# Attention beside an MLP: two steps at a time, with projections and turned output in one stretch of the TensorE and all transposes in another

## The chip, the cores and the metric

The kernel runs on one core of a Trainium2 chip. The metric is the device time of one execution in microseconds. Five engines work side by side, each through its own instructions in order: TensorE (PE) multiplies, VectorE (DVE), ScalarE (ACT) and GpSimd (POOL) do the rest of the arithmetic, and SyncE (SP) issues nearly all DMA transfers. Matmul results land in PSUM, which has eight banks of 128 x 512 floats. POOL does not touch PSUM here.

## The reference, cut to what matters

```python
def phi(x):                                   # random features of one row of q or k
    proj = einsum('bhsd,md->bhsm', x, omega)
    h = proj - sum(x * x) / 2
    return exp(h - max(h)) / sqrt(m)
kv  = einsum('bhsm,bhsd->bhmd', phi(k), v)
z   = sum(phi(k), axis=2)
num = einsum('bhsm,bhmd->bhsd', phi(q), kv)
den = einsum('bhsm,bhm->bhs', phi(q), z) + 1e-06
x   = (num / den) as [B * S, H * D]
out = (silu(x @ w_gate) * (x @ w_val)) @ w_out
```

There are 8 batches, 8 heads, 576 rows, head width 64, 128 features; the MLP has 4608 tokens, width 512 and inner width 1536. Everything is fp32.

## The kernel before, in words

The heads are taken in pairs, so that 128 partitions hold two heads. The rows of a batch are nine groups of 256. A *step* `n` takes two groups: one of q and one of k, but only k in the first six steps and only q in the last six (66 to 71). There are 72 steps, and 4 more in which the last results come out.

A step goes through these stages, several steps apart, and the program's names are used in the profile too:

- `st_transpose`: four transposes (`pt`) turn the loaded rows (`nat`), ACT copies them to `x`; POOL squares them (`sq`).
- `st_project`: `pp`, eight matmuls with 64 rows each, for two heads that lie in the two halves of the array's rows. Two tiles, one for each head, take two PSUM banks.
- `st_max`: DVE sums `sq`, takes the maxima of `pp` and makes the bias (`st`). `st_exp`: ACT takes eight exponentials from `pp` to `ph`.
- `k_accumulate`: `kvacc` sums phi(k) x v in one bank; at a batch's half `kv_finalize` copies it to `kvr` and, from batch 4 on, transposes z (`zp`), which goes to DRAM (`zd`) and comes back to all partitions (`zt`).
- `q_transpose`: `ptq`, four transposes of phi(q), copied to `qt`.
- Batches 0 to 3: `q_mult` makes `po` (numerator and denominator), DVE divides (`xn`), `q_out` transposes that to `xt`. Batches 4 to 7: POOL and DVE make the denominator from `zt` (`jk`, `dj`), POOL divides phi(q) (`q_norm`), and `q_out` makes `xt` at once as *turned output*, from two matmuls of 64 columns in the two halves of the array's columns.
- ACT copies `xt` out: to the MLP's input `xh`/`xl`, or through `xo` and a DMA to DRAM (`xs`).

From step 25 on (`EARLY`) the MLP runs beside this. Its matmuls (`g`, `v`, `o`, 128 x 128 x 512, three for each product of split numbers) are given out in shares: `course` says how much of it is due by each step, and each `SHARE` in the list of a step gives an equal part of what is due. Before, the list for one step is `GROUPED`, with six shares. A scheduler settles the final order on each engine; the lists give it the program's order.

PSUM is held by pools: `ps_m` three banks (`ps_moe`), `ps_p` two (`ps_proj`), and one each for `ps_a` (`ps_att`), `ps_b` (`ps_tr`) and `ps_k` (`kvacc`). In the stretch beside the MLP, `pp` is in `ps_proj`, `pt` in `ps_tr`, `ptq` and `xt` in `ps_att` or `ps_tr`, `po` and `zp` in `ps_att`.

After step 75 these pools are given back and the rest of the MLP runs alone (`pair_rounds`), from about 565 us of the span to its end.

Of the kernel before, what the change touches and what calls it, by code (L numbers as in the profile page):

```python
# [24 lines left out]
def kernel(  # L25
# [404 lines left out]
    def st_transpose(n):  # L430
        if n >= NS:
            return
        nat = nats.pop(n)
        pt = ps_tr(f"pt_{n}", [P, 2, G])
        for i in range(2):
            for c in range(CH):
                turned_in[:] = [
                    transpose(
                        pt[:, i, c * P : (c + 1) * P], nat[:, i, c].rearrange("p h d -> p (h d)"), ident
                    )  # L440
                ]
        x = att.tile([P, 2, G], F32, name=f"x_{n}", tag="x")

        st = att.tile([P, 4, 2, CH, 2], F32, name=f"st_{n}", tag="st", bufs=6)
        sq = att.tile([P, 2, CH, 2, D], F32, name=f"sq_{n}", tag="sq")
        nc.gpsimd.tensor_tensor(sq, nat, nat, op=ALU.mult)  # L446
        if 3 <= n < EARLY:
            nc.scalar.copy(x[:, 0], pt[:, 0])
            nc.vector.tensor_copy(x[:, 1], pt[:, 1])
            for w in (D // 2, D // 4):  # L450
                lower_, upper_ = (sq[..., o : o + w].rearrange("p i c h d -> p (i c h) d") for o in (0, w))
                nc.gpsimd.tensor_tensor(lower_, lower_, upper_, op=ALU.add)
        else:
            nc.scalar.copy(x, pt)  # L454
# [42 lines left out]
    def st_exp(n):  # L497
        if n >= NS:
            return
        st, _, pp = sts.pop(n)  # L500
        for i, (kind, b, g) in enumerate(steps[n]):
            ph = att.tile([P, CH, 2 * M], F32, name=f"ph{i}_{n}", tag=f"ph{i}", bufs=3)
            for hh in range(2):
                for c in range(CH):
                    step_end["s"] = nc.scalar.activation(  # L505
                        ph[:, c, hh * M : (hh + 1) * M], pp[hh][:, i, c, :],
                        AF.Exp, bias=st[:, 3, i, c, hh : hh + 1], scale=1.0,
                    )
            box[kind, b, g] = ph
        return True  # L510
# [7 lines left out]
    def kv_finalize(b, a2):  # L518
        acc = kvacc.pop((b, a2))
        raw = att.tile([P, 4, VW], F32, name=f"kvr{b}_{a2}", tag="kvr", bufs=4)  # L520
        nc.scalar.copy(raw, acc)  # L521
        for j in range(2):
            kvst[b, 2 * a2 + j] = raw[:, 2 * j : 2 * j + 2, :]
        if b >= BPOOL:

            zp = ps_att(f"zp{b}_{a2}", [4, P])
            transpose(zp, raw[:, :, D], ident)
            zs = att.tile([4, P], F32, name=f"zs{b}_{a2}", tag="zs")
            nc.scalar.copy(zs, zp)
            zd = dram.tile([4, P], F32, name=f"zd{b}_{a2}", tag="zd", bufs=4)  # L530
            nc.sync.dma_start(zd, zs)
            zds[b, a2] = zd

    zds = {}
    zbc = {}

    def load_z(n):
# [12 lines left out]
    def q_den(n):  # L550

        n -= JLAG
        for _, b, g, gr in slots(n, "q"):
            if b < BPOOL:
                continue
            ph = box["q", b, g].rearrange("p c (h m) -> p c h m", m=M)
            jk = att.tile([P, CH, 2, M], F32, name=f"jk{b}_{g}", tag="jx")
# [12 lines left out]
            dn = att.tile([P, 3, CH, 2], F32, name=f"dj{b}_{g}", tag="dj", bufs=6)  # L570
# [51 lines left out]
    def q_transpose(n):  # L622
# [2 lines left out]
        todo += [(b, g) for _, b, g, gr in slots(n - NLAG, "q") if b >= BPOOL]  # L625
        for i, (b, g) in enumerate(todo):
            ph = box.pop(("q", b, g))
            pt = (ps_moe if m < EARLY else ps_tr if i else ps_att)(f"ptq{b}_{g}", [P, 2, G])
            for hh in range(2):
                for c in range(CH):  # L630
                    transpose(pt[:, hh, c * P : (c + 1) * P], ph[:, c, hh * M : (hh + 1) * M], ident)
# [3 lines left out]
    def q_mult(n):  # L635

        n -= MLAG
        for _, b, g, gr in slots(n, "q"):
            if b >= BPOOL:
                continue  # L640
            qt = qts.pop((b, g))
            po = ps_att(f"po{b}_{g}", [P, CH, 2, VW])
# [14 lines left out]
            xn = att.tile([P, CH, 2, D], F32, name=f"xn{b}_{g}", tag="jx")  # L657
            nc.vector.tensor_tensor(
                xn.rearrange("p c h d -> p (c h) d"),
                po[:, :, :, 0:D].rearrange("p c h d -> p (c h) d"),  # L660
# [10 lines left out]
    cols_done = [0]  # L671

    def q_out(n):
        n -= OLAG
        for i, b, g, gr in slots(n, "q"):
            po = (ps_att if n + OLAG < EARLY or i else ps_tr)(f"xt{b}_{g}", [P, G])
            first = column(b, gr)
            if b < BPOOL:
                xn = xns.pop((b, g))
# [2 lines left out]
            else:  # L682
# [437 lines left out]
    def turn_next(n):  # L1120
# [17 lines left out]
    GROUPED = (
        q_out,
        st_project,  # L1140
        q_transpose,
        lambda n: k_accumulate(n, 0),
        lambda n: k_accumulate(n, 1),
        st_max,
        st_exp,
        q_den,
        lambda n: st_transpose(n + 1),
        SHARE,
        SHARE,
        SHARE,  # L1150
        lambda n: q_norm(n + 1),
        q_mult,
        SHARE,
        SHARE,
        SHARE,
    )

    for n in range(2):
# [8 lines left out]
    warm(2, turned_in[0])  # L1167
    loaded = 3
    ends = []
    for n in range(NN):  # L1170
        if loaded <= n + LA:
            load(loaded)
            loaded += 1
# [6 lines left out]
        want = OPS * np.interp(clock[n + 1], [clock[m] for m, _ in marks], [x for _, x in marks])  # L1180
        order = CLOSE if n < EARLY else GROUPED
        left = len(order) if n < EARLY else order.count(SHARE)
        for what in order:
            with ExitStack() as es:
                if n < EARLY:
                    for ins in ends if what is st_project else ends[:1]:
                        es.enter_context(tc.issue_after(ins.ins))
                if what is not SHARE:
                    what(n)
            if n < EARLY:  # L1190
                if what is st_project:
                    ends.clear()
                ends.append(newest_pe[0])
            if what is turn_next and n < 2:
                warm(2, turned_in[0])
            if n < EARLY or what is SHARE:
                due = course[n + 1] - given[0] - debt[0]
                if due > 0:
                    give(due / left)
                for _ in range(int(np.ceil((want - ticks[0]) / left))):  # L1200
                    tick()
                left -= 1
# [42 lines left out]
```

## Time and profile before

| | |
|---|---|
| median of 3 runs | 1166.98 us (1164.1 to 1167.11) |
| profiled execution | 1166.82 us, span 1165.0 us |
| PE busy | 1137.2 us, 98% of the span |
| DVE, ACT, POOL busy | 61%, 58%, 53% |
| granted TensorE clock, mean | 0.997 |
| attention alone | 0 to about 112 us |
| attention beside the MLP | about 112 to 565 us |
| MLP alone | about 565 to 1165 us |

In a timeline of PE, each row is a run of equal matmuls: start, length, line, tiles and count. The end of a matmul is modelled and overlaps the next; so the distance from one start to the next is the cost, not the length. An fp32 matmul that isn't a transpose is shown as two. In a list of waits, the first name waited for the second.

### The profile page before, as it was taken

The page shows a single profiled execution, that of the slowest core. Times are in us where ns is not written, and L with a number is a line of the kernel's source. Part 1 is how long each engine was busy: PE and PEld are TensorE (multiplying, and loading weights), DVE is VectorE, ACT ScalarE, POOL GpSimd, SP SyncE. Part 2 cuts the span into 40 slices and gives each one's busy share as a digit, 9 for nine tenths or more (in the row PEclk, how much of TensorE's full clock was granted, in tenths as well). Part 3 has the DMA queues.
Part 4 walks back from the last instruction along what each step waited for, and adds up shares of the span by engine and source line. Part 5 has one row for each costly group of instructions (what it writes and reads, how often), then busy time and mean ns, then how long its engine had stood idle before and what let it go on. Part 6 is the DMA issues. An engine that isn't in the chain of part 4 may idle for free.

```text
span 1165.0 us, 18915 instructions
## 1 busy us (share of the span) xinstructions
PE 1137.2 (98%) x6645; PEld 939.5 (81%) x6646; DVE 707.4 (61%) x1289; ACT 678.3 (58%) x1539; POOL 615.5 (53%) x559
## 2 busy tenths in 40 slices
PE   8999999999999999989999999999999999999998
PEld 6888888888878778867788778888878888888886
DVE  5787667455656656565474566665566666456654
ACT  5887886876776866757434544454544445444441
POOL 5664433344556675587245555544455543455551
PEclk9999999999999999999999999999999999999999
DMA  6764445655445642322544111124211111211103
GB/s 137 179 160 114 128 142 161 178 135 143 122 126 137 168 132 78 114 68 65 154 118 126 46 55 55 55 74 122 59 55 55 54 37 46 81 55 55 46 19 72
DMA packets 173966, 114.30 MB, mean 98 GB/s; under 512 B 125840, under 2 KB 144304, under 8 KB 173872
## 3 DMA queue, kind: packets, MB, share of 16 engines
q1 hardware_dynamic: 172528, 112.78, 35.5%
q8 instruction: 52, 0.85, 0.3%
q10 hardware_dynamic: 1344, 0.33, 0.1%
q14 instruction: 42, 0.34, 0.1%
HBM read 87.88 MB, written 25.18 MB: 97 GB/s over the span
## 4 chain that ended last, share of the span: by engine, by line
PE 74%; DVE 10%; ACT 6%; POOL 4%; DMA 3%; issue 2%; SPq 1%; ACTq 0%; POOLq 0%; DVEq 0%
PE o L103 22%; PE a L103 16%; PE c L103 8%; PE g L103 6%; PE pp L103 4%; PE v L103 4%; PE d L103 4%; PE kvacc L103 3%; ACT ph L505 3%; PE ptq L107 2%; PE po L103 2%; PE pt L107 2%; PE xt L103 1%; DVE st L490 1%; POOL wlo L264 1%
## 5 line engine op out<-in xcount | busy, mean ns | idle before, releaser
L505 ACT ACTIVATE ph<-pp,st 128x128 f32<-128x128 f32 x576 | 157.8, 386 | 26.5 <-DVE st L493 26.0
L763 DVE TENSOR_TENSOR acc<-o,acc 128x512 f32<-128x512 f32 x156 | 105.8, 684 | 94.6 <-PE o L103 94.3
L446 POOL TENSOR_TENSOR sq<-nat 128x512 f32<-128x512 f32 x72 | 78.2, 1086 | 130.5 <-DVE st L483 89.1
L950 POOL TENSOR_TENSOR wlo<-wspare,whi 128x512 fp32r<-128x512 f32 (+1 forms) x60 | 61.0, 1037 | 117.4 <-ACT whi L949 111.0
L490 DVE TENSOR_REDUCE st<-pp 128x4 f32<-128x512 f32 x144 | 92.5, 683 | 39.0 <-PE pp L103 38.7
L264 POOL TENSOR_TENSOR wlo<-wraw,whi 128x512 fp32r<-128x512 f32 x59 | 82.7, 1406 | 26.7 <-ACT whi L263 22.8
L103 PE MATMUL pp<-omT,x 64*128 64x128 f32 x1152 | 87.3, 285 | 3.2 <-ACT x L454 2.2
L103 PEld LDWEIGHTS pp<-omT,x 64*128 64x128 f32 x1152 | 72.6, 187 | 20.2 <-issue 11.2
L950 POOL TENSOR_TENSOR wlo<-s,whi 128x512 fp32r<-128x512 f32 x64 | 82.6, 1311 | 3.8 <-ACT whi L949 3.8
L1059 ACT COPY late<-a 128x512 f32<-128x512 f32 x72 | 42.2, 586 | 59.7 <-PE a L103 58.5
L103 PE MATMUL o<-whi,late 128*128 128x512 f32 x192 | 74.5, 389 | 0.0
L571 DVE TENSOR_REDUCE dj<-jk 128x4 f32<-128x512 f32 x36 | 24.6, 684 | 73.5 <-POOL jk L567 60.6
L103 PE MATMUL kvacc<-v,ph 128*128 128x65 f32 x512 | 65.9, 268 | 0.5 <-ACT kvr L521 0.5
L824 POOL TENSOR_TENSOR hl<-sl,hh 128x512 fp32r<-128x512 f32 x36 | 47.0, 1308 | 34.8 <-ACT hh L823 34.7
L103 PEld LDWEIGHTS kvacc<-v,ph 128*128 128x128 f32 x512 | 63.1, 192 | 0.8 <-ACT kvr L521 0.6
L1063 DVE TENSOR_TENSOR late<-c,late 128x512 f32<-128x512 f32 x25 | 17.3, 692 | 69.7 <-PE c L103 60.6
L103 PE MATMUL g<-xh,whi 128*128 128x512 f32 x144 | 59.4, 412 | 0.0
L103 PE MATMUL o<-whi,hh 128*128 128x512 f32 x144 | 58.5, 406 | 0.1
L303 POOL TENSOR_TENSOR wc<-st 128x512 int32<-128x512 int32 x36 | 37.5, 1042 | 39.6 <-DVE st L298 17.2
L103 PE MATMUL v<-xh,whi 128*128 128x512 f32 x144 | 57.9, 402 | 0.0
L103 PE MATMUL g<-xh,wlo 128*128 128x512 f32 x144 | 57.7, 401 | 0.0
L103 PE MATMUL g<-xl,whi 128*128 128x512 f32 x144 | 57.2, 397 | 0.0
(261 smaller groups left out, 3369.4 us busy)
## 6 DMA issues: line engine op xcount, KB each, us to landing
wraw<-wscr SPq DMA_DIRECT2D x63, 256.0 KB, 2.7
wspare<-wscr SPq DMA_DIRECT2D x60, 256.0 KB, 2.8
wscr<-wc SPq DMA_DIRECT2D x36, 256.0 KB, 2.2
out_dram<-acc SPq DMA_DIRECT2D x72, 128.0 KB, 2.4
nat<-in_k_dram SPq DMA_DIRECT2D x64, 128.0 KB, 3.0
nat<-in_q_dram SPq DMA_DIRECT2D x64, 128.0 KB, 3.1
v<-in_v_dram SPq DMA_DIRECT2D x62, 128.0 KB, 3.5
st<-in_moe_w_gate_dram SPq DMA_DIRECT2D x12, 512.0 KB, 4.1
```

The costliest lines, as they stand in the source:

```text
L103: newest_pe[:] = [nc.tensor.matmul(*args, **kw)]
L107: newest_pe[:] = [nc.tensor.transpose(*args, **kw)]
L264: nc.gpsimd.tensor_tensor(lo, raw, hi.bitcast(F32), op=ALU.subtract)
L303: nc.gpsimd.tensor_tensor(ui, ri, low, op=ALU.add)
L446: nc.gpsimd.tensor_tensor(sq, nat, nat, op=ALU.mult)
L490: nc.vector.tensor_reduce(st[:, 1, :, :, hh], pp[hh], axis=AX.X, op=ALU.max, negate=True)
L505: step_end["s"] = nc.scalar.activation(ph[:, c, hh * M : (hh + 1) * M], pp[hh][:, i, c, :], AF.Exp, bias=st[:, 3, i, c, hh : hh + 1], scal ...
L571: nc.vector.tensor_reduce(dn[:, 0], jk, axis=AX.X, op=ALU.add)
L763: nc.vector.tensor_tensor(a_, po, a_, op=ALU.add)
L824: nc.gpsimd.tensor_tensor(hl, h, hh.bitcast(F32), op=ALU.subtract)
L950: nc.gpsimd.tensor_tensor(lo, src_, hi.bitcast(F32), op=ALU.subtract)
L1059: newest["s"] = nc.scalar.copy(keep[name], ps)
```

## The change

From step 25 on, two steps are done at a time, by one list `DOUBLE` with twelve shares in place of two times `GROUPED` with six. In it:

- `st_project` of both steps stands behind the output `xt` of two steps (`q_out_both`), with quarters of `k_accumulate` around it. `xt` goes to the MLP's banks (`ps_moe`), two groups in one bank.
- The transposes stand in a second stretch, seven shares later: `ptq`, `pt`, `ptq`, `pt`, for steps `n + 2` and `n + 3`.
- The banks: the first step's `pp` takes `ps_att` and `ps_tr`, the second's takes both of `ps_proj`. The transposes take the same four banks afterwards. `po` of the second step moves to `ps_tr`.
- `zp` is no longer made in `kv_finalize` but in `z_rows`, after the seventh share, in a bank of `ps_moe`; `load_z` follows at once.
- The loads of both steps are issued at the start of the pair (`loads`).
- In SBUF `st` has 4 buffers and not 6, `ph0` (q) 4 and not 3, `dj` 4 and not 6; `jk` and `xn` no longer share two buffers but have 1 and 2; `zs` has 1.
- The list before step 25, `CLOSE`, loses its last `q_out` and makes one more `st_transpose`.

```diff
-        pt = ps_tr(f"pt_{n}", [P, 2, G])
+        pt = (ps_proj if n > EARLY + 1 and (n - EARLY) % 2 else ps_tr)(f"pt_{n}", [P, 2, G])
...
-        new = ps_moe if n < EARLY and n % 2 else ps_proj
-        pp = [new(f"pp{hh}_{n}", [P, 2, CH, M]) for hh in range(2)]
+        if n < EARLY:
+            new = (ps_moe, ps_moe) if n % 2 else (ps_proj, ps_proj)
+        else:
+            new = (ps_proj, ps_proj) if (n - EARLY) % 2 else (ps_att, ps_tr)
+        pp = [new[hh](f"pp{hh}_{n}", [P, 2, CH, M]) for hh in range(2)]
...
-            pt = (ps_moe if m < EARLY else ps_tr if i else ps_att)(f"ptq{b}_{g}", [P, 2, G])
+            new = (ps_att, ps_tr) if (m - EARLY) % 2 == 0 else (ps_proj, ps_att)
+            pt = (ps_moe if m < EARLY else new[i])(f"ptq{b}_{g}", [P, 2, G])
...
+    def q_out_both(n):
+        groups = slots(n - 1 - OLAG, "q") + slots(n - OLAG, "q")
+        at = []
+        for k_, g_ in enumerate(groups):
+            if k_ % 2 == 0:
+                two = ps_moe(f"xt{g_[1]}_{g_[2]}", [P, 2, G])
+            at.append((g_, two[:, k_ % 2]))
+        place_out(at)
...
+    DOUBLE = (
+        (lambda n: k_accumulate(n, 0), 0),
+        (q_out_both, 0),
+        (st_project, 0),
+        (st_project, 1),
+        (lambda n: k_accumulate(n, 1), 0),
+        (q_norm, 0),
+        (st_max, 0),
+        (st_exp, 0),
+        (q_den, 0),
+        (st_max, 1),
+        (st_exp, 1),
+        SHARE,
+        SHARE,
+        SHARE,
+        (q_norm, 1),
+        SHARE,
+        SHARE,
+        SHARE,
+        SHARE,
+        (lambda n: z_rows(), 0),
+        (load_z, 0),
+        (load_z, 1),
+        (lambda n: k_accumulate(n, 0), 1),
+        (q_transpose, 0),
+        (st_transpose, 2),
+        (q_transpose, 1),
+        (st_transpose, 3),
+        (lambda n: k_accumulate(n, 1), 1),
+        SHARE,
+        SHARE,
+        (q_mult, 0),
+        (q_mult, 1),
+        SHARE,
+        SHARE,
+        SHARE,
+        (q_den, 1),
+    )
...
+    for n in range(EARLY, NN, 2):
+        loads(n)
+        loads(n + 1)
+        left = DOUBLE.count(SHARE)
+        last = min(n + 2, NN)
+        for what in DOUBLE:
+            if what is not SHARE:
+                what[0](n + what[1])
+                continue
+            share(course[last] - given[0] - debt[0], wanted(last), left)
+            left -= 1
```

On PE, before, around step 57 (batch 5). `v_6` is a unit of the MLP of twelve matmuls, `xt_3` the turned output of an earlier step, `pp_57` the projections, `ptq_4` the transposes of an earlier phi(q), `pt_5429` those of the next step's rows. Lines that repeat are left out.

```order
L103 MATMUL v_6_5361<-xh_737,wlo_1_5033 128x512
L103 MATMUL xt_3_5378<-qt_3_5303,kvr_1_4542 64x256 [waits Activation_49]
...
L103 MATMUL pp_57_5387<-omT,x_5335 128x128 [waits DVE_49,Activation_49]
L103 MATMUL pp_57_5388<-omT,x_5335 128x128 [waits DVE_49,Activation_49]
...
L107 MATMUL ptq_4_5397<-ident,ph_55_5198 128x128 [waits Pool_49]
...
L103 MATMUL kvacc_1_5080<-v_103,ph_55_5203 128x65 [waits DMAHW6_49]
...
L107 MATMUL pt_5429<-ident,nat_5159 128x128 [waits DMAHW2_49,PE_49,Activation_49]
...
L103 MATMUL v_7_5447<-xh_737,whi_1_5129 128x512
```

The same place now. At the dots after `pp_58` stand, besides the rest of the projections, a quarter of `k_accumulate` and `v_7` and `v_8`, 24 matmuls of the MLP.

```order
L103 MATMUL kvacc_1_5110<-v_103,ph_55_5201 128x65 x2
L103 MATMUL xt_2_5371<-qt_2_5291,kvr_1_4545 64x256 [waits DVE_49,Activation_49]
...
L103 MATMUL xt_2_5371<-qt_3_5308,kvr_1_4545 64x256 [waits Activation_49]
...
L103 MATMUL pp_57_5388<-omT,x_5298 128x128 [waits PE_49]
L103 MATMUL pp_57_5389<-omT,x_5298 128x128 [waits PE_49]
...
L103 MATMUL pp_58_5398<-omT,x_5315 128x128 [waits Activation_49]
L103 MATMUL pp_58_5399<-omT,x_5315 128x128 [waits PE_49]
...
L107 MATMUL ptq_4_5509<-ident,ph_55_5196 128x128 [waits DVE_49,Activation_49,Pool_49]
...
L107 MATMUL pt_5516<-ident,nat_5142 128x128 [waits DMAHW3_49,DMAHW4_49,DVE_49,Activation_49]
...
L107 MATMUL ptq_5_5526<-ident,ph_56_5217 128x128 [waits DVE_49,Activation_49,Pool_49]
...
L107 MATMUL pt_5533<-ident,nat_5358 128x128 [waits DMAHW4_49,DVE_49,Activation_49]
```

What moved: the transposes no longer follow the projections at once, the projections of two steps follow each other with nothing between, and the transposes wait for ACT and DVE to be done with the banks of those projections.

On ACT, now, in the same pair of steps: the copies of the transposes stand behind all sixteen exponentials.

```order
L508 ACTIVATE ph_57_5416<-pp_57_5388,st_5299 128x128 [waits DVE_49,PE_49]
...
L508 ACTIVATE ph_58_5437<-pp_58_5398,st_5316 128x128 [waits DVE_49,PE_49]
...
L508 ACTIVATE ph_58_5442<-pp_58_5398,st_5316 128x128 [waits PE_49]
...
L846 CAST hh_7_5488<-sl_7_5229 128x512 [waits DVE_49]
...
L644 COPY qt_4_5514<-ptq_4_5509 128x512 [waits PE_49]
L454 COPY x_5521<-pt_5516 128x512 [waits PE_49]
...
L644 COPY qt_5_5531<-ptq_5_5526 128x512 [waits PE_49]
L454 COPY x_5538<-pt_5533 128x512 [waits PE_49]
```

Before, eight exponentials stand between the copies of one step and those of the next; now sixteen do, and four copies follow together.

More of the change, by code (lines that the diff above doesn't have):

```diff
@@ L442, in st_transpose @@
         x = att.tile([P, 2, G], F32, name=f"x_{n}", tag="x")
-        st = att.tile([P, 4, 2, CH, 2], F32, name=f"st_{n}", tag="st", bufs=6)
+        st = att.tile([P, 4, 2, CH, 2], F32, name=f"st_{n}", tag="st", bufs=4)
         sq = att.tile([P, 2, CH, 2, D], F32, name=f"sq_{n}", tag="sq")
@@ L501, in st_exp @@
         for i, (kind, b, g) in enumerate(steps[n]):
-            ph = att.tile([P, CH, 2 * M], F32, name=f"ph{i}_{n}", tag=f"ph{i}", bufs=3)
+            ph = att.tile([P, CH, 2 * M], F32, name=f"ph{i}_{n}", tag=f"ph{i}", bufs=4 - i)
             for hh in range(2):
@@ L524, in kv_finalize, with z_rows @@
         if b >= BPOOL:
-            zp = ps_att(f"zp{b}_{a2}", [4, P])
+            zraw[b, a2] = raw
+    zraw = {}
+    zds = {}
+    def z_rows():
+        for (b, a2), raw in zraw.items():
+            zp = ps_moe(f"zp{b}_{a2}", [4, P])
             transpose(zp, raw[:, :, D], ident)
-            zs = att.tile([4, P], F32, name=f"zs{b}_{a2}", tag="zs")
+            zs = att.tile([4, P], F32, name=f"zs{b}_{a2}", tag="zs", bufs=1)
             nc.scalar.copy(zs, zp)
@@ L532, in kv_finalize @@
             zds[b, a2] = zd
-    zds = {}
+        zraw.clear()
     zbc = {}
@@ L556, in q_den @@
             ph = box["q", b, g].rearrange("p c (h m) -> p c h m", m=M)
-            jk = att.tile([P, CH, 2, M], F32, name=f"jk{b}_{g}", tag="jx")
+            jk = att.tile([P, CH, 2, M], F32, name=f"jk{b}_{g}", tag="jx", bufs=1)
             if gr is None:
@@ L569, in q_den @@
                 )
-            dn = att.tile([P, 3, CH, 2], F32, name=f"dj{b}_{g}", tag="dj", bufs=6)
+            dn = att.tile([P, 3, CH, 2], F32, name=f"dj{b}_{g}", tag="dj", bufs=4)
             nc.vector.tensor_reduce(dn[:, 0], jk, axis=AX.X, op=ALU.add)
@@ L641, in q_mult @@
             qt = qts.pop((b, g))
-            po = ps_att(f"po{b}_{g}", [P, CH, 2, VW])
+            odd = n + MLAG >= EARLY and (n + MLAG - EARLY) % 2
+            po = (ps_tr if odd else ps_att)(f"po{b}_{g}", [P, CH, 2, VW])
             for c in range(CH):
@@ L656, in q_mult @@
             nc.vector.reciprocal(dn[:, 1], dn[:, 0])
-            xn = att.tile([P, CH, 2, D], F32, name=f"xn{b}_{g}", tag="jx")
+            xn = att.tile([P, CH, 2, D], F32, name=f"xn{b}_{g}", tag="xn")
             nc.vector.tensor_tensor(
@@ L673, in q_out, with place_out @@
     def q_out(n):
-        n -= OLAG
-        for i, b, g, gr in slots(n, "q"):
-            po = (ps_att if n + OLAG < EARLY or i else ps_tr)(f"xt{b}_{g}", [P, G])
+        place_out([(g_, (ps_att if n < EARLY else ps_tr)(f"xt{g_[1]}_{g_[2]}", [P, G])) for g_ in slots(n - OLAG, "q")])
+    def q_out_both(n):
[6 more added lines that the diff above has]
+        place_out(at)
+    def place_out(at):
+        for (i, b, g, gr), po in at:
             first = column(b, gr)
@@ L691, in q_out @@
                         )
+        for (i, b, g, gr), po in at:
+            first = column(b, gr)
             j, o = tile_of(first)
@@ L712, in q_out @@
                 cols_done[0] = first + (RES if gr is None else G)
-        return bool(slots(n, "q"))
     def mm1(ps, wts, xs):
@@ L1134 @@
         q_den,
-        lambda n: n == EARLY - 1 and q_out(n),
         lambda n: n == EARLY - 1 and q_mult(n),
+        lambda n: n == EARLY - 1 and st_transpose(n + 2),
     )
[L1138 to L1147, printed above, removed]
+    DOUBLE = (
[10 more added lines that the diff above has]
+        (st_exp, 1),
         SHARE,
@@ L1150 @@
         SHARE,
-        lambda n: q_norm(n + 1),
-        q_mult,
+        (q_norm, 1),
         SHARE,
@@ L1169, with loads @@
     ends = []
-    for n in range(NN):
+    def loads(n):
+        nonlocal loaded
         if loaded <= n + LA:
@@ L1179, with share, wanted @@
             load_raw(0)
[L1180 to L1183, printed above, removed]
-            with ExitStack() as es:
[L1185 to L1193, printed above, removed]
+    def share(due, want, left):
+        if due > 0:
+            give(due / left)
+        for _ in range(int(np.ceil((want - ticks[0]) / left))):
+            tick()
+    def wanted(n):
+        return OPS * np.interp(clock[n], [clock[m] for m, _ in marks], [x for _, x in marks])
+    for n in range(EARLY):
+        loads(n)
+        for at, what in enumerate(CLOSE):
+            with ExitStack() as es:
+                for ins in ends if what is st_project else ends[:1]:
+                    es.enter_context(tc.issue_after(ins.ins))
+                what(n)
+            if what is st_project:
+                ends.clear()
+            ends.append(newest_pe[0])
             if what is turn_next and n < 2:
                 warm(2, turned_in[0])
[L1196 to L1202, printed above, removed]
-        load_z(n)
+            share(course[n + 1] - given[0] - debt[0], wanted(n + 1), len(CLOSE) - at)
+        load_z(n)
+    for n in range(EARLY, NN, 2):
+        loads(n)
+        loads(n + 1)
[7 more added lines that the diff above has]
+            left -= 1
     late.close()
```

## The prediction

> **What bounds the kernel now.** I read the page's busy times first, then busy time by stretch, then a timeline of PE over one step, then the waits.
>
> ```profile
> span 1165.0 us, 18915 instructions
> PE 1137.2 (98%) x6645; PEld 939.5 (81%) x6646; DVE 707.4 (61%) x1289; ACT 678.3 (58%) x1539; POOL 615.5 (53%) x559
> PE 74%; DVE 10%; ACT 6%; POOL 4%; DMA 3%; issue 2%; SPq 1%; ACTq 0%; POOLq 0%; DVEq 0%
> ```
> ```profile
> 112.00:508.00 396.00, 389.61 (x2690) 320.21 (x2689) 236.52 (x508) 289.86 (x701) 212.68 (x186) 1.00 0.49 134
> 508.00:565.00 57.00, 51.11 (x333) 37.81 (x332) 30.25 (x58) 35.13 (x84) 39.70 (x37) 1.00 0.21 59
> ```
>
> The columns of the second are the stretch, its length, and busy time of PE, weight loads, DVE, ACT and POOL. PE is the bound in the stretch that changes: 440.7 of 453 us. Its idle time there is 6.4 + 5.9 = 12.3 us; ACT, the next, is busy 72% of it (weight loads overlap the matmuls). So the change is worth what it takes from PE's own work, plus or minus what it does to those 12.3 us. The MLP alone after 565 us keeps its work, and attention's end simply moves it.
>
> PE's work contains time that no wait shows. One step with turned output:
>
> ```profile
> 410.16 0.39 PE L103 MATMUL v<-xh,wlo 128*128 128x512 f32 x1
> 410.47 0.65 PE L103 MATMUL xt<-qt,kvr 128*64 128x256 f32 x4
> 411.06 1.16 PE L103 MATMUL pp<-omT,x 64*128 64x128 f32 x16
> 412.15 0.66 PE L107 MATMUL ptq<-ident,ph 128*128 128x128 f32 x4
> 412.64 1.00 PE L103 MATMUL kvacc<-v,ph 128*128 128x65 f32 x8
> 413.48 0.61 PE L107 MATMUL pt<-ident,nat 128*128 128x128 f32 x4
> 413.84 0.48 PE L103 MATMUL v<-xh,whi 128*128 128x512 f32 x1
> ```
> ```profile
> 409.93 0.39 PE L103 MATMUL v<-xl,whi 128*128 128x512 f32 x1
> 411.72 0.50 PE L103 MATMUL pp<-omT,x 64*128 64x128 f32 x6
> 411.94 0.28 PE L103 MATMUL pp<-omT,x 64*128 64x128 f32 x2
> ```
> ```profile
> PEld pp L103 <- issue: 11.2, 41, 0.4
> PEld xt L103 <- issue: 8.1, 23, 0.4
> ```
>
> The second fence shows moments inside the first. The MLP's matmuls start 0.23 us apart (409.93 to 410.16), but `xt` starts 0.31 after: 0.08 for turning to two column halves. Projections run in pairs, one for each row half: 411.72 to 411.94 is two pairs, 0.11 each. From 411.06 to 411.72 there are five pairs in 0.66, 0.11 too much, and the last pair lasts to 412.15, 0.21: 0.10 too much. So a set of projections pays 0.21 for turning in and out. `ptq` takes 0.49 for four, where 0.11 each (the `pt` that follow `kvacc` without a turn: 0.36 to the next unit) makes 0.44: 0.05. `xt` takes 0.59 for two pairs twice as wide, by estimate 2 x 0.22: 0.15, part of it the change from columns to rows. The sum is 0.08 + 0.21 + 0.05 + 0.15 = **0.49 us a step**. The weight loads show the same: they were held 41 and 23 times by nothing but "issue", at these turns.
>
> With transposed output (batches 0 to 3), `xt` needs no turn:
>
> ```profile
> 192.15 0.38 PE L107 MATMUL xt<-ident,xn 128*128 128x128 f32 x2
> 192.46 1.16 PE L103 MATMUL pp<-omT,x 64*128 64x128 f32 x16
> 193.55 0.66 PE L107 MATMUL ptq<-ident,ph 128*128 128x128 f32 x4
> 194.04 1.00 PE L103 MATMUL kvacc<-v,ph 128*128 128x65 f32 x8
> ```
>
> `xt` to `pp` is 0.31 where two transposes need 0.22 (0.09), `pp` again 1.09 (0.21), `ptq` 0.49 (0.05): **0.35 us**.
>
> **The change, part by part.**
>
> *Turns.* A pair of steps now enters the columns once, goes to the rows once, and leaves them once; the second step's first projections follow the first's last ones without a turn. One set of turns of two goes. Nothing shows `kvacc` before `xt`, or after `pp` here; `kvacc` may pay the 0.05 that `ptq` paid, so a pair saves 0.40 to 0.49 with turned output (I take 0.45) and 0.30 to 0.35 without (0.33). Steps 45 to 70 are 13 pairs of the first kind, 25 to 44 ten of the second: 13 x 0.45 + 10 x 0.33 = **9.2 us**, ends 8.2 and 9.9.
>
> *Projections that miss their partner.* When the two heads' matmuls aren't issued alternately, they follow one another:
>
> ```profile
> 112.00:545.00 433.00, 58.24 (x752) 48.28 (x752) 60.30 (x94) 103.53 (x379) 1.00 0.46 128
> 410.00:413.00 3.00, 1.16 (x16) 0.97 (x16) 0.75 (x2) 0.00 (x0) 1.00 0.14 40
> ```
>
> This is busy time of `pp` alone: 47 steps at 1.16 would be 54.5, so 3.7 us is lost in a few steps. In the new order all alternate but those of step 25, eight unpaired: 8 x 0.11 = 0.9, and 0.3 for its split `xt`. Saved: **2.5 us** (0 to 3.7, since part of the 3.7 is waiting).
>
> *Waits that go.*
>
> ```profile
> PE ptq L107 <- ACT xo L703: 2.9, 4, 2.1
> PE xt L107 <- DVE xn L658: 2.3, 2, 1.2
> PE zp L107 <- ACT kvr L521: 2.0, 3, 1.1
> PE pt L107 <- ACT qt L633: 1.9, 1, 1.9
> ...
> PE pt L107 <- ACT xo L703: 0.7, 2, 0.4
> ```
>
> `ptq` and `pt` waited for a single bank that held `xt` or the last `ptq`; `zp` waited because it followed `kvr`'s copy in line. `xt` is in the MLP's banks now and `zp` comes later. That is 7.5 us; I count 5 as gone, since the last steps, with two q's, still queue four `ptq` behind ACT's copies.
>
> *Waits that come.* The transposes take the banks of the projections, so DVE and ACT must have emptied them. Durations:
>
> ```profile
> 412.25 1.29 DVE L490 TENSOR_REDUCE st<-pp 128x4 f32<-128x512 f32 x2 [0.97 <-PE pp L103]
> 413.57 0.17 DVE L492 SCALAR_TENSOR_TENSOR st<-st 128x8 f32<-128x8 f32 x1
> 413.77 0.17 DVE L493 SCALAR_TENSOR_TENSOR st<-st 128x8 f32<-128x8 f32 x1
> 413.86 0.68 DVE L483 TENSOR_REDUCE st<-sq 128x8 f32<-128x512 f32 x1
> ```
> ```profile
> 414.12 0.59 ACT L454 COPY x<-pt 128x512 f32<-128x512 f32 x1 [0.70 <-PE pt L107]
> 414.61 2.18 ACT L505 ACTIVATE ph<-pp,st 128x128 f32<-128x128 f32 x8
> ```
>
> Count from the first projection. The first maximum starts at 1.1 (before: 412.25 - 411.06 = 1.19, less a turn), the bias is ready 1.7 later, at 2.8; then `sq` 0.7, and the second step's maxima and bias 1.7: 5.2. Its exponentials take 0.27 each: six free the bank of the second `ptq`, at 6.8; eight the last, at 7.4. PE meanwhile does 16 pairs (1.9), a turn and two quarters of `k_accumulate` (1.0), the MLP, and before the second `ptq` another 0.9 of transposes. In the new order the MLP's part is mostly 21 to 36 matmuls and once 18: 0.23 each, 4.8 to 8.3 (4.1). PE arrives at 8.6 or later (7.9): a margin of 1.8 us, in one pair 1.1. What stands before the exponentials on ACT eats into this: a function table or an `x` copy. If the sixteen are late, `ptq` and everything behind it on PE waits, then `qt`, `x` and the next projections.
>
> Other covers: `xt` in `ps_moe` must be copied out before the MLP's next-but-one unit; 1.9 us of projections and 0.5 of `kvacc` cover two copies (0.4 each). The second step's rows load only at its pair's start:
>
> ```profile
> nat<-in_k_dram SPq DMA_DIRECT2D x64, 128.0 KB, 3.0
> ```
> ```profile
> SPq L307 <- POOL wc L303: 84.9, 30, 6.6
> ```
>
> They are needed about 9 us later and land 3.0 after issue; but SP issues in order, behind stores that waited up to 6.6. Were that to happen at the wrong moment, 1 us is lost. `zd` and `zt` now stand together on SP, four times, ahead of loads. `xn` must follow `po` within two or three shares, ten times. The smaller rings (`st`, `dj`, `jk`, `zs`) are reused a full pair later at the earliest, except `jk`, which makes POOL wait for DVE's sum (0.68), with POOL 56% busy. I put all new waits at 0.3 us a pair, 23 x 0.3 = 7 us, between nothing and the 1 us a pair of the rival below.
>
> *Sum.* -9.2 - 2.5 - 5 + 7 = -9.7. The profiled execution, 1166.82 (0.16 under the median), gives **1157.1 us**.
>
> **Rivals.**
>
> *The exponentials come late, slower.* If the sixteen stall PE by 1 us a pair, beyond their margin by a table load or a blocked copy, 23 us come in place of 7: 1166.8 - 16.7 + 23 = 1173; at 1.5 us, 1185. It is slower by more than 0.3% from (16.7 + 3.5)/23 = 0.9 us a pair. For it: ACT is already 72% busy here. Against: the margin counted above. Waits cost more when they cluster:
>
> ```profile
> 421.77:425.19 3.42, 1.99 (x16) 1.58 (x15) 2.44 (x5) 3.23 (x8) 3.08 (x4) 1.00 0.61 210
> 425.19:428.60 3.41, 3.41 (x10) 2.64 (x9) 2.38 (x4) 2.66 (x10) 2.38 (x3) 0.50 0.57 138
> ```
>
> After 3.4 us in which PE was busy for 1.99, the granted clock was 0.5 for the next 3.4, worth 3.41 / 2 = 1.7 us. Three such clusters are 5 us. The Trainium skill ("TensorE: Matmul & The Clock Gate", HAM oscillation) asks only that PE have no idle gap over about 3.4 us; by that, waits of 1 us would cost themselves alone and these 5 us would not come. The trace disagrees: no gap there was that long.
>
> *The saved time is given back as waits.* Idle rises from 12.3 to about 20 us: 1166.8 - 11.7 + 8 = 1163 to 1167.
>
> *The turn isn't saved.* If the 0.11 at a set's start belongs to its weights and not to the turn, only 0.08 + 0.10 a pair goes: 23 x 0.18 + 2.5 = 6.6, with +2 of waits 1162. Against it: `pt` after `kvacc` has new weights and pays nothing.
>
> *Waits vanish too.* If seven shares cover all, -9.2 - 2.5 - 7.5 = 1147.6.
>
> **How the numbers follow.** Likeliest 0.55: the turns and pairs save, waits stay about as they were, 1151 to 1163.4 by the ends 0 and 15 of the waits. Waits vanish 0.13 (below 1151), turn not saved 0.07 (1162), given back 0.14 (within 0.3%, 3.5 us, about what a measurement of this kernel can tell from no change), late exponentials 0.11. Faster is 0.55 + 0.13 + 0.07 = 0.75, same 0.14, slower 0.11. The range 1147 to 1168 leaves out the slow rival and a few of the fast.
>
> **What would show it.** In a timeline of PE two sets of `pp`, 32 matmuls, should last 1.97 and not 2 x 1.09; holds by "issue" at `pp` should fall from 41 to about 25, busy time of `pp` by some 3 us. PE's idle time in the stretch should stay near 12 us, with waits of `ptq` or `pt` for `ph` in place of `xo`. If those pass 15 us, or half-clock stretches multiply, the prediction is wrong.

## The result, and the profile after

The change made the kernel slower: a median of 1186.6 us (1186.1 to 1188.2, 4 runs) against 1166.7 us (1164.1 to 1167.1, 4 runs), a ratio of 1.018 with a 95% interval of 1.016 to 1.020. The forecast of 1157 us was wrong, and on the wrong side. The profiled execution took 1188.2 us.

The busy times on the page after, and the shares of the chain of waits:

```profile
span 1186.4 us, 18959 instructions
PE 1135.5 (96%) x6646; PEld 951.0 (80%) x6646; DVE 700.0 (59%) x1289; ACT 663.8 (56%) x1531; POOL 613.6 (52%) x559
PE 69%; DVE 10%; ACT 8%; POOL 5%; DMA 4%; issue 3%; SPq 0%; ACTq 0%; POOLq 0%; DVEq 0%
```

PE's busy time hardly fell, its share of the chain fell from 74 to 69%, and ACT's, POOL's and DMA's rose. The same stretches as before; attention now ends at 588 and not at 565 us (columns: length, busy time of PE, weight loads, DVE, ACT, POOL, then the granted clock):

```profile
112.00:508.00 396.00, 370.57 (x2578) 315.52 (x2578) 223.82 (x489) 261.55 (x658) 192.81 (x172) 0.97 0.47 129
508.00:588.00 80.00, 71.94 (x461) 57.36 (x460) 35.40 (x77) 49.81 (x122) 55.50 (x51) 0.98 0.24 68
```

PE's idle time in the first stretch was 6.4 us and is 25.4, and the clock, 1.00 before, is 0.97.

**The turns are saved.** One pair on PE, then the holds of weight loads by "issue", then busy time of `pp` alone over the part beside the MLP:

```profile
466.28 1.08 PE L103 MATMUL xt<-qt,kvr 128*64 128x256 f32 x8
467.30 2.06 PE L103 MATMUL pp<-omT,x 64*128 64x128 f32 x32
469.28 0.66 PE L103 MATMUL kvacc<-v,ph 128*128 128x65 f32 x4
```
```profile
PEld pp L103 <- issue: 6.4, 22, 0.8
PEld xt L103 <- issue: 4.4, 9, 1.3
```
```profile
112.00:580.00 468.00, 51.31 (x752) 46.42 (x752) 60.50 (x94) 102.58 (x380) 0.97 0.44 120
```

The 32 projections take 1.98 us, the holds fell from 41 and 23 to 22 and 9, and `pp` lost 6.9 us of busy time.

**The waits came elsewhere.** Who PE waited for, beside the MLP (total, number, longest; other rows left out at the dots):

```profile
PE kvacc L103 <- ACT kvr L524: 9.6, 2, 5.4
PE ptq L107 <- POOL sq L446: 5.0, 3, 2.7
PE ptq L107 <- POOL ph L593: 2.9, 2, 2.1
PE ptq L107 <- POOL jk L577: 2.3, 1, 2.3
...
PE ptq L107 <- ACT qt L644: 2.1, 2, 1.5
...
PE ptq L107 <- ACT ph L508: 1.7, 3, 0.9
```

And on ACT, the waits for a store of `xo` and for weights, now, and the store's row before:

```profile
ACT xo L727 <- DMA xs<-xo: 19.0, 8, 4.5
...
ACT whi L263 <- DMA wraw<-wscr: 11.2, 4, 6.1
...
ACT wc L289 <- POOL wlo L264: 7.6, 3, 3.5
```
```profile
ACT xo L703 <- DMA xs<-xo: 1.2, 1, 1.2
```

Most of PE's waiting is in few and long waits. Three of them, the first two read on several engines. First a pair at 420 us, SP, ACT, DVE and PE in turn:

```profile
419.41 2.60 SPq L388 DMA_DIRECT2D nat<-in_k_dram  x4
422.05 0.59 SPq L553 DMA_DIRECT2D zt<-zd  x1
422.74 2.26 SPq L728 DMA_DIRECT2D xs<-xo  x3
426.33 0.32 SPq L728 DMA_DIRECT2D xs<-xo  x1
```
```profile
420.91 0.66 ACT L727 COPY xo<-xt 128x192 f32<-128x192 f32 x3
426.09 0.21 ACT L727 COPY xo<-xt 128x64 f32<-128x64 f32 x1 [4.52 <-DMA xs<-xo]
426.20 2.18 ACT L508 ACTIVATE ph<-pp,st 128x128 f32<-128x128 f32 x8
429.81 2.18 ACT L508 ACTIVATE ph<-pp,st 128x128 f32<-128x128 f32 x8 [1.43 <-PE ptq L107]
```
```profile
428.76 0.69 DVE L581 TENSOR_REDUCE dj<-jk 128x4 f32<-128x512 f32 x1 [3.33 <-POOL jk L577]
429.56 0.16 DVE L496 SCALAR_TENSOR_TENSOR st<-st 128x8 f32<-128x8 f32 x1
```
```profile
431.57 0.63 PE L107 MATMUL ptq<-ident,ph 128*128 128x128 f32 x4 [1.37 <-POOL sq L446]
```

Two steps' outputs cross a border of the MLP's tiles, so four copies to `xo` come at once, with three buffers. The first store is issued only at 422.74, as four loads of a rest group (the last 64 rows of all four head pairs) and `zt` stand ahead of it on SP. The fourth copy waits 4.52 us, and the exponentials wait behind it. POOL's `jk` needs the first eight exponentials, DVE's `dj` needs `jk`, and the second step's bias stands behind `dj` on DVE: so the second eight start only at 429.81, and the second `ptq` is late. The list gives `ptq` as what released the exponentials, but the bias was done at the same time (429.56 + 0.16). It gives `sq` as what released the second `ptq`; in the trace `sq` ended at 431.49 and the sixth of the exponentials, after which the bank of that `ptq` is free, at 431.47; the third wait below tells which of them it was.

Then a pair at 389 us, ACT, POOL and PE:

```profile
394.51 0.66 ACT L289 ACTIVATE wc<-st 128x512 f32<-128x512 f32 x1 [3.48 <-POOL wlo L264]
395.07 0.36 ACT L524 COPY kvr<-kvacc 128x260 f32<-128x260 f32 x1
395.32 0.59 ACT L644 COPY qt<-ptq 128x512 f32<-128x512 f32 x1
```
```profile
391.22 1.04 POOL L593 TENSOR_TENSOR ph<-ph,dj 128x512 f32<-128x512 f32 x1 [0.41 <-DVE dj L583]
393.21 1.26 POOL L264 TENSOR_TENSOR wlo<-wraw,whi 128x512 fp32r<-128x512 f32 x1
```
```profile
386.44 1.00 PE L103 MATMUL kvacc<-vrest,ph 128*128 128x65 f32 x8
395.49 0.90 PE L103 MATMUL kvacc<-vrest,ph 128*128 128x65 f32 x3 [5.38 <-ACT kvr L524]
```

The sum in `kvacc` was done at 387.3, but its copy `kvr` stood on ACT behind a weight conversion (`wc`), which waited for a buffer that POOL's `wlo` had to free, and POOL had worked on late products of attention before. PE stood for 5.38 us.

The third, at 362 us on ACT: a weight's cast waited 6.11 us for its load and a function table followed, while the sixteen exponentials stood behind both. The two `ptq` of that pair waited 2.67 and 0.94 us. The list names `sq` for these too, but the first `ptq` started at 366.42, with `sq` done at 365.69. In the trace both started 0.10 us after the sixth exponential of their step ended (366.32 and 368.39), and so did the one at 431.57.

```profile
362.73 0.62 ACT L263 CAST whi<-wraw 128x512 fp32r<-128x512 f32 x1 [6.11 <-DMA wraw<-wscr]
363.37 1.28 ACT L508 ACT_TABLE_LOAD   x1
364.66 4.24 ACT L508 ACTIVATE ph<-pp,st 128x128 f32<-128x128 f32 x16
```

What follows the wait at 389 us, by windows of 3.41 us (the clock is the number after the five busy times):

```profile
388.80:392.21 3.41, 1.31 (x8) 0.80 (x6) 1.37 (x3) 2.20 (x3) 3.00 (x3) 1.00 0.14 29
392.21:402.45 10.24, 6.96 (x24) 5.81 (x26) 0.86 (x2) 4.49 (x9) 3.54 (x4) 0.50 0.54 147
```

10.2 us at half clock. Beside the MLP there are five such stretches now, 27.3 us together, and there was one of 3.4.

**The account.** All of attention lies before the MLP's 1400th matmul. The time at which that starts, split: waits are the distances between starts on PE above 0.6 us, from 100 us on, less the 0.23 of an MLP matmul each; half clock is half the length of its stretches; the rest is PE's own work.

| | 1400th matmul | waits | half clock | rest |
|---|---|---|---|---|
| before | 642.5 | 14.3 (15) | 1.7 | 626.5 |
| after | 663.9 | 39.0 (27) | 13.7 | 611.2 |
| difference | +21.4 | +24.7 | +12.0 | -15.3 |

So PE's own work fell by more than was forecast. Where a wait lies inside a half-clock stretch, as at 392 us, the table counts its time in both columns, so 15.3 is too much. By kinds of matmul, from 112 us on, each up to the next start, distances above 0.6 us counted as 0.23 and half clock taken out of the others, the work fell by 13.4 us: `pp` 54.9 to 47.7, `xt` 27.6 to 24.2, `ptq` 25.9 to 24.2, the MLP 330.3 to 325.7, while `pt` rose from 18.8 to 21.0. Waits below 0.6 us are not told apart from work here.

### The profile page after: what moved, and what is told of

The parts are those of the page before. It is cut to its first block, busy times and chain, and to the rows that moved or that the text cites. A ratio compares the mean times of both kernels' runs of the same rounds, so it can differ in the third digit from the quotient of the medians.

```text
span 1186.4 us, 18959 instructions
## 1 busy us (share of the span) xinstructions
PE 1135.5 (96%) x6646; PEld 951.0 (80%) x6646; DVE 700.0 (59%) x1289; ACT 663.8 (56%) x1531; POOL 613.6 (52%) x559
## 4 chain that ended last, share of the span: by engine, by line
PE 69%; DVE 10%; ACT 8%; POOL 5%; DMA 4%; issue 3%; SPq 0%; ACTq 0%; POOLq 0%; DVEq 0%
PE o L103 21%; PE a L103 15%; PE c L103 7%; PE v L103 5%; PE pp L103 4%; PE d L103 4%; PE kvacc L103 4%; ACT ph L508 3%; PE g L103 3%; PE po L103 2%; DVE st L493 2%; PE pt L107 1%; PE ptq L107 1%; PE xt L103 1%; DMA xs<-xo 1%
## 5 line engine op out<-in xcount | busy, mean ns | idle before, releaser
L103 PE MATMUL pp<-omT,x 64*128 64x128 f32 x1152 | 80.4, 285 | 1.7 <-ACT x L454 1.7
L103 PEld LDWEIGHTS kvacc<-v,ph 128*128 128x128 f32 x512 | 69.6, 194 | 10.9 <-ACT kvr L524 5.2
L103 PE MATMUL kvacc<-v,ph 128*128 128x65 f32 x512 | 73.1, 271 | 4.7 <-ACT kvr L524 4.7
L581 DVE TENSOR_REDUCE dj<-jk 128x4 f32<-128x512 f32 x36 | 24.7, 685 | 64.7 <-POOL jk L577 49.8
L107 PE MATMUL ptq<-ident,ph 128*128 128x128 f32 x288 | 44.4, 279 | 14.0 <-POOL sq L446 5.0
```

What stands on the lines that cost most here:

```text
L103: newest_pe[:] = [nc.tensor.matmul(*args, **kw)]
L107: newest_pe[:] = [nc.tensor.transpose(*args, **kw)]
```

## The experiments

The theory: the turns are saved, as shown above, but two steps' work now comes at once to ACT, DVE and POOL, which work in order through small rings; a long wait there (a store, a weight buffer, a sum) stands ahead of the exponentials or of `kvr`, PE waits, and the clock adds half as much again. The rival: sixteen exponentials and four transposes are simply too close, whatever stands ahead.

The intervals of the single edits are wide against what each brings: `ring` and `dj` lie clear of the changed kernel, `kvr` just touches it, and `jk` can't be told from it.

| kernel | median us (runs) | ratio to before (95%) |
|---|---|---|
| changed | 1186.6 (4) | 1.018 (1.016 to 1.020) |
| `ring` | 1180.3 (4) | 1.013 (1.010 to 1.015) |
| `kvr` | 1181.6 (4) | 1.014 (1.012 to 1.016) |
| `dj` | 1180.1 (4) | 1.013 (1.011 to 1.015) |
| `jk` | 1184.5 (4) | 1.016 (1.015 to 1.018) |
| `three`: ring, kvr, dj | 1174.6 (4) | 1.008 (1.006 to 1.010) |
| `five`: those and jk | 1169.4 (8) | 1.0035 (1.002 to 1.005) |
| `six`: `five` and conversions moved | 1165.1 (10) | 0.9995 (0.998 to 1.001) |
| `single`: before, with ring, kvr, dj | 1166.5 (10) | 1.000 (0.999 to 1.002) |
| `cover`: changed, 9 and 3 shares | 1208.0 (4) | 1.036 (1.034 to 1.037) |
| `eight`: `six`, 8 and 4 shares | 1173.8 (4) | 1.006 (1.004 to 1.008) |
| `fewer`: `six`, 6 and 6 shares | 1177.6 (6) | 1.009 (1.006 to 1.012) |
| `zlate`: `six`, `z_rows` behind the transposes | 1165.4 (10) | 1.000 (0.999 to 1.001) |
| `zfewer`: `zlate` and `fewer` | 1177.9 (4) | 1.010 (1.008 to 1.012) |
| `one`: `six`, `dj` held in steps with one q | 1168.9 (7) | 1.003 (1.002 to 1.004) |
| `zone`: `one` and `z_rows` a share later | 1167.5 (11) | 1.001 (1.000 to 1.002) |
| `spread`: before, stalls apart | 1227.9 (4) | 1.052 (1.050 to 1.055) |
| `cluster`: before, stalls in threes | 1193.0 (4) | 1.022 (1.020 to 1.024) |

**Four edits, one at a time** (shortened).

```diff
-tag="xo", bufs=3)        # ring
+tag="xo", bufs=4)        # NVF = 7 makes the room
-nc.scalar.copy(raw, acc)           # kvr, in kv_finalize
+nc.vector.tensor_copy(raw, acc)
-nc.vector.tensor_reduce(dn[:, 0], jk, axis=AX.X, op=ALU.add)    # dj
+with tc.issue_after(biased[0].ins):     # and (q_den, 0) behind (st_exp, 1)
+    nc.vector.tensor_reduce(dn[:, 0], jk, axis=AX.X, op=ALU.add)
-jk: tag="jx", bufs=1; xn: tag="xn"      # jk
+jk and xn: tag="jx"
```

> The changed kernel with four buffers for xo in place of three (v's tiles 7 in place of 8 to make room). Theory (work that stands ahead of the exponentials and of kvr in ACT's order): the 19.0 us in which ACT waited for the store of xo nearly go; PE's late ptq at 431.6 us (1.4) and what followed it at 440.2 us (4.2, and the half clock of 6.8 us behind it) go or shrink: about 1180 us, 1176 to 1184. Rival (two steps' sixteen exponentials and the four transposes are simply too close, whatever stands ahead): 1186 to 1187.

Measured 1180.3, as the theory had it: ACT waits 2.8 us for stores of `xo`, in place of 19.0.

> The changed kernel with kvr copied by DVE in place of ACT. Theory: kvacc's two waits of 9.6 us in all for kvr, which stood behind a weight conversion on ACT, go, and with them the half-clock stretches of 10.2 and 6.8 us (8.5 us lost): up to 18 us; a part comes back as waits for qt or x, which stay behind the same conversion: about 1174 us, 1169 to 1181. Rival (the exponentials' lateness sets the time): no more than 3 us, 1184 to 1187. Rival (half clock has nothing to do with these waits): 1177, with the half-clock stretches still there.

Measured 1181.6, between theory and rival: `kvacc` waits 2.2 us in place of 9.6, and half clock fell from 27.3 to 17.1 us, but `xt` waits 4.5 us in place of 2.5, and one `ptq` 4.1, where the longest had been 2.7.

> The changed kernel with DVE's sum for the denominator (dj) held behind the second step's bias, so that the bias no longer waits for POOL's jk of the first step's phi(q). Theory: the late ptq at 431.6 and 530.3 us (1.4 and 2.1 us) shrink: 1182 to 1185 us. Rival (dj only takes its place in a queue that is late anyway): 1186 to 1187; a third way, dj and so q_norm later, ptq's waits for ph longer: 1188 or more.

Measured 1180.1, a larger gain than the theory asked. But now POOL waited 15.0 us for `dj` between its `jk`, with one buffer: a ring that had not been felt.

> The changed kernel with jk and xn sharing two buffers again, as before the change, in place of one for jk and two for xn. Theory (every engine's place in line is set by small rings): POOL's product jk no longer waits for DVE's sum of the last one, so q_norm and the ptq behind it come earlier: 1180 to 1184 us. Rival (jk's ring is off the path; in the changed kernel ptq waited for q_norm's ph only 2.9 us in all): 1186 to 1187.

Measured 1184.5, between the two, and not clear of noise: the 2.1 us are not shown.

**Together.**

> The changed kernel with all three edits: four xo buffers, kvr by DVE, dj behind the second bias. Theory: -6 - 12 - 3 = 1166 us if they add, 1163 to 1172, about as fast as before the change; half-clock stretches in the part beside the MLP fall from 27 us to 10 or less. Rival (sixteen exponentials too close to the transposes): 1180 or more, with ptq still late by about 1 us in most pairs.

Measured 1174.6, a miss: of 17.8 us that the three brought alone, 12.0 remain. PE now waits most for POOL's division of phi(q) (`q_norm`, the norm below), and POOL's `jk`, with its one buffer, for DVE's `dj`, 21.8 us in all (PE's waits, then POOL at 529 us):

```profile
PE ptq L107 <- POOL ph L594: 12.3, 9, 3.3
```
```profile
529.47 1.28 POOL L577 TENSOR_TENSOR jk<-ph,zt 128x512 f32<-128x512 f32 x1 [2.89 <-DVE dj L582]
```

> The kernel with four xo buffers, kvr by DVE and dj behind the second bias, and besides two buffers for jk and xn. In that kernel without the last edit ptq waited 12.3 us in all for q_norm's ph, and POOL waited for DVE's dj by 0.9 to 2.9 us a time. Theory: half or more of these 12.3 us go: 1165 to 1170 us. Rival (POOL's own work, not the ring, makes q_norm late): 1173 to 1176.

Measured 1169.4. With `dj` held, two `jk` buffers bring 5.3 us, where alone they brought nothing measurable; the wait for the norm only fell to 11.4, but `kvacc`'s of 3.4 and `xt`'s of 2.4 went, and the half-clock stretches fell from 13.7 to 3.4 us.

```diff
-for _ in range(int(np.ceil((want - ticks[0]) / left))):      # six, in share
-    tick()
+if left <= 5 or left > 9 or loaded <= EARLY:
+    for _ in range(int(np.ceil((want - ticks[0]) / left))):
+        tick()
```

> As the one with two jk buffers, and besides no weight conversion is given out in the four shares ahead of the transposes. Theory: the long wait of kvacc for kvr (3.4 us and the half clock of 6.8 us behind it), which came from a conversion that stood ahead on ACT and DVE and waited for POOL's wlo, goes: 3 to 6 us less than with it, 1161 to 1167. Rival (the conversions are only moved to where they hold up something else): within 2 us of it.

Measured 1165.1, 4.3 less, but not for the reason given: the wait of `kvacc` had gone in `five` already, and the profiles of the two, 1.0 us apart at the MLP's 1400th matmul, don't show where 4.3 come from. Taken together, five edits that leave the two stretches as they are bring back the 21 us that the change cost; so the pairs' closeness alone, whatever stands ahead, doesn't account for the loss. The same places in line cost nothing where steps come singly:

> The kernel before the change, one step at a time, with the edits that helped the changed one: four xo buffers, kvr by DVE, dj behind the step's bias (jk has two buffers there already). Theory (the rings and places in line hurt only where two steps' work comes at once): 1163 to 1168 us, as before. Rival (they would be worth as much there, and the pairs gain nothing by themselves): 1155 to 1160.

Measured 1166.5, as before the change: the loss is that of the pairs together with these rings and places in line; neither costs it alone.

**Margin.** Shares moved from behind the transposes to ahead of them, two in the changed kernel (`cover`) and one with the five edits (`eight`), and one the other way (`fewer`).

```diff
         SHARE,
+        SHARE,          # eight; cover: two of them
         (lambda n: z_rows(), 0),
...
         (q_mult, 1),
         SHARE,
         SHARE,
-        SHARE,
```

> The changed kernel with nine shares of the MLP between projections and transposes and three behind, in place of seven and five. If the sixteen exponentials merely lack a margin of 1 to 2 us in many pairs, two more shares (about 2 us of MLP) remove most of the 14 us in which ptq waited: 1174 to 1180 us. If ACT and POOL are blocked for 3 to 5 us in a few pairs (stores, weight rings), the long waits stay, and the copies of qt and x have less cover: 1183 to 1190.

Measured 1208.0, far above both. PE's longest waits there:

```profile
PE xt L103 <- ACT qt L644: 9.3, 2, 8.2
PE ptq L107 <- POOL ph L593: 7.3, 3, 4.0
PE kvacc L103 <- ACT kvr L524: 5.5, 1, 5.5
```

Now `xt` waits for ACT's copies, up to 8.2 us, and 54.6 us ran at half clock, while all of `ptq`'s waits only fell from 14.0 to 12.6 us. So two more shares ahead removed little of the lateness there; that the copies are late for want of the shares behind them is the likely reason, not one that was shown apart.

> The changed kernel with all five edits (xo, kvr, dj, jk, no conversions ahead of the transposes), and eight shares ahead of the transposes and four behind. If what is left there, ptq's 9.9 us of waits for q_norm's ph (ten of about 1 us), is a lack of margin: half of it goes, 1158 to 1163 us. If the copies of qt, x and kvr lose their cover, as with nine and three shares in the changed kernel (21 us more): 1166 to 1180.

> The same five edits, and six shares ahead of the transposes and six behind. Nine and three cost 21 us in the changed kernel, eight and four 9 us with the five edits. If the copies of qt, x and kvr and the divisions are the shorter cover, the course goes on: 1158 to 1163 us. If the exponentials have no margin left: ptq waits for ph by another 0.5 to 1 us in most pairs, 1170 to 1185.

Measured 1173.8 and 1177.6: seven and five shares are the best of the three. In `eight`, `ptq` waits for the norm as in `six` (9.6 and 9.9 us), so that was no lack of margin; `po` waits more for ACT's copies (5.1 and 2.1 us), which doesn't explain all of the 9 us that it is slower than `six`. In `fewer`, `ptq` comes some 3 us late in five pairs, in `six` in two.

**Does the saved work show in the time?** In `six` the rest of the account is 613.2, nearly as small as the 611.2 after the change, with waits of 22.6 and half clock of 6.8: against before 13.3 saved, and 8.3 + 5.1 given back. I tried to take the last long waits away: `z_rows` and `load_z` at once behind the transposes (`zlate`) or a share later (`zone`), and `dj` free again where a step has two q's (`one`, `zone`).

```diff
-with tc.issue_after(biased[0].ins):
+with tc.issue_after(biased[0].ins) if len(slots(n, "q")) == 1 else ExitStack():
```

> The changed kernel with all five edits (xo, kvr, dj, jk, no conversions ahead of the transposes), and z_rows and load_z behind the transposes in place of ahead of them. There zp waited 2.9 us for a silu, as a bank of ps_moe had to come free, with ptq and the rest behind it and 3.4 us at half clock after it. If that wait is one of those that keep the saved turns from showing: 3 to 5 us less, 1160 to 1162 us. If another wait takes its place: 1164 to 1166.

> Both: z_rows behind the transposes, and six and six shares. If both waits are real and add: 1155 to 1160 us; otherwise near the worse of the two.

Measured 1165.4 and 1177.9: another wait took the place of the first, and the two don't add. In `zlate` the wait of `zp` for a silu went, and one of 2.4 us for `kvr`, at once ahead of it, came, with 6.8 us at half clock.

> The changed kernel with the five edits, but dj held behind the second bias only in steps with one q. In the last pairs, with two q's a step, DVE's held dj kept POOL's jk and with it q_norm late: there ptq waited 2.7 and 1.1 us at 510 us and 2.7 us at 531 us, with 6.8 us at half clock behind the first. Theory: most of these go: 1158 to 1162 us. Rival (POOL's own work of four products and four norms a pair sets it): 1164 to 1166.

> The same, and z_rows and load_z one share behind the transposes, so that zp waits neither for a silu (2.9 us, ahead of them) nor for kvr (2.4 us, at once behind them), each with 3.4 us or more at half clock after it. Theory: 3 to 5 us less than with z_rows ahead of the transposes, 1154 to 1158 us, faster than before the change. Rival: another wait takes its place, within 1.5 us of the other.

Measured 1168.9, worse than theory and rival, and 1167.5, within 1.5 us of the other, as its rival had it. In `one` the wait of `ptq` near 507 us, 2.7 us in `six`, is 3.5 and has another reason (ACT, DVE, and PE's waits from 500 to 512 us):

```profile
508.67 2.18 ACT L508 ACTIVATE ph<-pp,st 128x128 f32<-128x128 f32 x8 [4.74 <-DVE st L496]
```
```profile
506.45 0.69 DVE L582 TENSOR_REDUCE dj<-jk 128x4 f32<-128x512 f32 x1 [2.69 <-POOL jk L573]
508.40 0.16 DVE L496 SCALAR_TENSOR_TENSOR st<-st 128x8 f32<-128x8 f32 x1
```
```profile
PE ptq L107 <- ACT ph L508: 3.5, 1, 3.5
```

This is the block of the changed kernel again: with `dj` free, the bias stands behind it; with `dj` held, POOL and the norm are late. No kernel with the pairs was measurably faster than before the change. Whether some order keeps the 13 us stays open.

**The clock by itself.** In the kernel before, in the MLP alone, a tiny matmul waits for two maxima that DVE takes of the product just made.

```diff
+def hold(src, ps, start):
+    for j in range(2):
+        nc.vector.tensor_reduce(held[:, j : j + 1], src, axis=AX.X, op=ALU.max)
+    matmul(ps[0:2, 0:4], held, none, start=start, stop=False, skip_group_check=True)
+# spread: ahead of product 5 of each group; cluster: ahead of 5, 6 and 3 of every third visit
```

> The kernel before the change, with 24 added stalls of PE in the MLP alone, one each 16 us or so: ahead of one product DVE takes two maxima of 512 of the product just made, and a tiny matmul that adds nothing to the result waits for both. A maximum takes 0.65 us here (st<-pp, two in 1.29), so a stall is some 1.7 us, 41 us in all. Theory (the clock is granted by how busy PE was in a window of 3.4 us, so single waits of this size cost themselves alone): 1207 us, 1200 to 1212, with few or no half-clock stretches. Rival (every long wait costs clock): 1225 or more.

> The same 24 stalls, but in eight clusters of three, 1.4 us of matmuls between them. Theory: each cluster leaves PE busy less than half of a window, and one or two windows of 3.4 us at half clock follow: 8 x 1.7 to 8 x 3.4 = 14 to 27 us more than with the stalls spread, 1221 to 1234 us. Rival (the half clock in the changed kernel has nothing to do with its waits): within 3 us of the spread one.

Measured 1227.9 and 1193.0, the wrong way round, since the stalls weren't those that the edit was to make: in `spread` PE waited 11 times for `held`, 36.7 us in all, mostly some 2.8 us each; in `cluster` four times, 6.6 us. But `spread` answers the question: its waits stand alone, 31 us or more apart but for one pair, and behind nine of the eleven follows a half-clock stretch of 3.4 or 6.8 us, 41 us in all. One wait and its two windows:

```profile
756.10 0.19 PE L106 MATMUL c<-none,held 128*2 128x4 f32 x2 [2.81 <-DVE held L963]
```
```profile
753.29:756.70 3.41, 0.60 (x4) 0.53 (x5) 3.35 (x6) 1.75 (x4) 3.41 (x3) 1.00 0.23 77
756.70:760.11 3.41, 3.41 (x10) 2.63 (x9) 0.00 (x0) 1.26 (x3) 1.27 (x3) 0.50 0.74 227
```

36.7 of waits and 41 / 2 = 20.5 of half clock make 57 of the 61 us that it cost. So single waits bring half clock, and no cluster is needed.

## Why the prediction was wrong, by its own steps

- *Turns, -9.2, and unpaired projections, -2.5.* Right, and a little too small: some 13.4 us of PE's own work went, where 11.7 were forecast. `pp` lost 6.9 us of busy time, not 3, and the pair's 32 matmuls take 1.98 us, forecast 1.97.
- *Waits that go, -5.* The rows named (`ptq` and `pt` for `xo`, `zp` for `kvr`) are gone from PE's waits. Others took their place.
- *Waits that come, +7.* This step failed. Together with the last it allowed waits to grow by 2 us; they grew by 24.7. Its 0.3 us a pair was a choice between nothing and 1 us, read from no row. The margin of 1.8 us was counted with ACT and DVE free for the pair. It named "a table load or a blocked copy" and "were that to happen at the wrong moment, 1 us is lost", but priced them by their usual length. Blocks of 4.5 us (a store), 3.5 us (a weight buffer) and 6.1 us (a weight load) stood there. The two copies "0.4 each" were four with three buffers; SP was looked at for late loads, not for stores behind loads. DVE's `dj`, in line ahead of the second bias, was not seen. Nor was the largest row of all: `kvr`'s copy, which frees the only bank of `kvacc`, behind a weight conversion on ACT, 9.6 us.
- *The clock.* This failed with it: the forecast left the clock as it was, and a rival gave three stretches 5 us. Five, partly two or three windows long, took 13.7 us.
- *The slow rival* (1173 to 1185) was right in what is late and close in price: 1186.6. Its form was not: not 1 us in each of 23 pairs, but 39.0 us in 27 waits, 19.5 of it in six. Two shares more ahead of the transposes didn't help, as `cover` shows.
- *Signs.* That idle time would pass 15 us and half-clock stretches multiply was named as what would make it wrong; both came.
- *A slip in the chances.* Waits of 0 and 15 us give 1150.1 and 1165.1, not 1151 and 1163.4; those two are where the neighbouring cases begin. The forecast of 1157.1 doesn't rest on it.

## What to carry to other kernels

Work that is put together saves on the engine that bounds and doubles the burst on the others: before doing so, walk each in-order queue of a pair and count what of the burst fits each ring (four copies into three buffers), what stands ahead of the work PE waits for, and what that waits for in turn. Price a block by its longest wait in the profile, not by its usual one. A wait that emptied more than half of a clock window here mostly cost 1.7 us or more besides itself; one that left PE busy for 2.9 us of the window cost itself alone.

## What the runs showed of the hardware

In the traces the granted clock changes only on a fixed grid of 3.41 us. In the 19 traces, from 115 us to 8 us before PE's end, I took every window at full clock and PE's busy time in it:

| PE busy in the window | windows | followed by half clock |
|---|---|---|
| up to 1.4 us | 51 | 51 |
| 1.4 to 1.7 | 25 | 13 |
| 1.7 to 2.9 | 245 | 4 |
| above 2.9 | 5426 | 0 |

So in these traces half clock follows a window with PE busy for less than 1.4 to 1.7 us, some 45% of it, and the place of a wait on the grid decides: the last of `spread`, 3.0 us between starts, split between two windows, brought none. The four windows above 1.7 us remain unexplained; one is that of the kernel before at 421.77 us, with two distances of 0.57 and 1.41 us between starts, where 0.11 is usual for such matmuls. A window at half clock costs, by estimate, half its length, 1.7 us, if PE has work all through it; stretches were one to four windows long (13.7 us twice in `cover`). The Trainium skill ("TensorE: Matmul & The Clock Gate", Part 1) states a free-running window of 3413 ns, and the traces agree: the stretches after the change start 7, 14, 6 and 21 windows apart. The rule of the Trainium skill's same page that PE should have no idle gaps above some 3.4 us ("HAM oscillation") falls short of what the traces show: single gaps of 2.8 us were followed by half clock.
